# Loading operands already transposed by DMA in a two-problem attention kernel

## The chip, the cores and the metric

The kernel runs on one core of one Trainium2 chip. The metric is device time in microseconds for one launch of the whole program. A profile is one execution of the program recorded by the hardware profiler; its span runs from the first to the last instruction and its own measured time is a little longer.

## The reference, cut to what matters

Two independent problems share one launch. Each has 2048 tokens, 512 channels and 32 heads of 16 channels. Problem A is attention in four segments of 512 tokens with a causal mask inside the segment, mixed with a linear "memory" of all earlier segments. Problem B is plain attention over all 2048 tokens, without a mask.

```python
# A: q, k, v = x@wq, x@wk, x@wv, cut in N=4 segments of L=512; phi(t) = t+1 if t>0 else exp(t)
for s in range(N):
    qs, ks, vs = q[:, :, s], k[:, :, s], v[:, :, s]
    logits = einsum('bhqd,bhkd->bhqk', qs, ks) * Dh**-0.5 + mask
    a_dot = einsum('bhqk,bhkd->bhqd', softmax(logits), vs)
    a_mem = einsum('bhld,bhde->bhle', phi(qs), M) / (einsum('bhld,bhd->bhl', phi(qs), z)[..., None] + 1e-06)
    outs.append(g * a_mem + (1.0 - g) * a_dot)          # g = sigmoid(beta), one value per head
    M = M + einsum('bhld,bhle->bhde', phi(ks), vs)
    z = z + einsum('bhld->bhd', phi(ks))
a = concat(outs) @ wo_A
# B: q, k, v = split(x @ wqkv)
b = softmax(einsum('bhqd,bhkd->bhqk', q, k) * Dh**-0.5) @ v @ wo_B      # per head
return concatenate([a, b], axis=-1)
```

## The kernel before, in words

The work is cut into units: one unit is four heads by 512 query tokens. A has 32 units (4 segments by 8 head groups), B has 32 (4 query chunks by 8 head groups). The order is fixed in `useq`: the eight units of A's segment 0 first, then B's units with A's later segments spread between them.

In a unit, TensorE computes scores with keys on the partitions (a bank is 128 keys by 512 queries of one head), an exponential turns them into P, and TensorE multiplies P by V into one accumulator `acc`, where an extra column of ones in V gives the softmax denominator. `finalize` then transposes and divides.

The exponentials of B are shared between two engines. ScalarE takes tiles of two or three banks from the PSUM tiles `s_ps` (`act_tile_b`, line 752; A's masked tiles are in `act_tile_a`, lines 678 to 688). VectorE takes one bank at a time from the two PSUM banks `d_ps` (`dve_bank`, scores on line 793) and builds an approximation of the exponential in three terms: line 804 writes the first term into the tile `pD`, and line 770 adds constants to make the other two. So a bank on VectorE needs three P-times-V products (line 906) with V scaled three ways (`VD`), where a bank on ScalarE needs one.

The instruction order on every engine is written out at build time by a planner: a loop in `fast_path` keeps a model clock `c["t"]` for TensorE and others for ScalarE, VectorE and GpSimd, and emits whatever its model says can go next. Each engine then runs its own list strictly in order. `pick` moves a B bank from VectorE's list to ScalarE's when the model says VectorE is behind, so the split between the engines is a result of the planning. Projections and other side work are "chores" with due times, run through the two `d_ps` banks: `chore_q`, `chore_k`, `chore_v` (four matmuls each and one copy out by VectorE), `chore_out` (output projection), `chore_xT` (transposition of x), `chore_kphi`, `chore_macc` and `chore_am` (A's memory). When TensorE would idle, `flush` and `fill_idle` emit products with zeros.

The parts around the change:

- x is loaded in blocks of 128 tokens (`load_x`, tile `xin`, five buffers). `fill_xT` (line 298) transposes a block by four TensorE products with the identity into a `d_ps` bank, and line 320 copies two blocks at a time to `xT_b` or `xT_a`. This is done eight times for B and six times for A's segments 1 to 3; A's segment 0 is done at the start.
- For the memory, phi(K) is needed with tokens on the partitions. `chore_kphi` projects K a second time in that layout, four chores per segment for three segments (line 333 with `wk_a`), copies it to `kb16` (line 424), and runs ScalarE's exp (line 431) and three GpSimd operations to make `phik`.
- All of these loads and the stores of the output (line 514) are issued from SyncE's queue.
- At the start, TensorE's list has the projections of the first q and k, then the q projection for the next two head groups (line 330, which needs the rest of `wq_a`), and only then the first scores of A (line 678).
- `PDB` is the number of `pD` buffers (3), and `QT_a`, the masked q of A, has three buffers.

Of the kernel before, what the change touches and what calls it, by code (L numbers as in the profile page):

```python
# [10 lines left out]
ALU = mybir.AluOpType  # L11
# [8 lines left out]
P = 128  # L20
# [21 lines left out]
def fast_path(ctx, tc, nc, A_x, A_wq, A_wk, A_wv, A_wo, A_beta, B_x, B_wqkv, B_wo, out, flag):  # L42
# [11 lines left out]
    PDB, PTB, XB = 3, 4, 5  # L54
# [13 lines left out]
    wv_b = sb_.tile([P, 4, D], BF16, name="wv_b", tag="phik", bufs=1)  # L68
# [3 lines left out]
    xorder = [("a", i) for i in range(4)] + [("b", i) for i in range(NSB)] + [("a", i) for i in range(4, NSB)]  # L72
    xtiles = {}
    xstate = dict(n=0)

    def load_x(upto, engs=(nc.sync,)):
        while xstate["n"] < min(upto, len(xorder)):
            k, i = xorder[xstate["n"]]
            xin = sb_.tile([P, D], BF16, name="xin", tag="xin", bufs=XB)
            src = xa2 if k == "a" else xb2  # L80
            engs[xstate["n"] % len(engs)].dma_start(out=xin[:], in_=src[i * P:(i + 1) * P, :])
            xtiles[(k, i)] = xin
            xstate["n"] += 1

    load_x(4, (nc.sync, nc.scalar))
# [46 lines left out]
    seg_v(0)  # L132
    beta_t = const.tile([P, HG], BF16, name="beta_t")
# [44 lines left out]
    load_x(5)  # L178
    nc.sync.dma_start(out=wv_b[:], in_=wview(B_wqkv)[:, :, 2 * D:3 * D])
    nc.sync.dma_start(out=wk_b[:], in_=wview(B_wqkv)[:, :, D:2 * D])  # L180
    nc.sync.dma_start(out=wq_b[:], in_=wview(B_wqkv)[:, :, 0:D])
# [104 lines left out]
    kphi_n = {}  # L286
    phik_t, phik_n, phik_at, mbd_at = {}, {}, {}, {}
# [7 lines left out]
    def fill_xT(bank, k, sbs):  # L295
        for n, i in enumerate(sbs):
            for cc in range(4):
                nc.tensor.transpose(bank[:, (4 * n + cc) * P:(4 * n + cc + 1) * P],  # L298
                                    xtiles[(k, i)][:, cc * P:(cc + 1) * P], ident[:])
        pe(60.0 * 4 * len(sbs), "full")  # L300

    def xT_tile(k, s):
        if (k, s) not in xT_t:
            if k == "a":
                xT_t[(k, s)] = sb_.tile([P, 4, 4, P], BF16, name="xT_a", tag="xT_a", bufs=1)
            else:
                for q in range(4):
                    xT_t[(k, q)] = None
                big = const.tile([P, NSB, 4, P], BF16, name="xT_b")
                for q in range(4):  # L310
                    xT_t[(k, q)] = big[:, 4 * q:4 * q + 4]
        return xT_t[(k, s)]

    def chore_xT(k, i0):
        load_x(xorder.index((k, i0)) + 2)
        bank = d_bank(BF16)
        c["t"] = max(c["t"], d_when())
        fill_xT(bank, k, (i0, i0 + 1))
        xt = xT_tile(k, i0 // 4)
        nc.vector.tensor_copy(xt[:, i0 % 4:i0 % 4 + 2], bank.rearrange("p (n c s) -> p n c s", n=2, c=4))  # L320
        d_done(dve_do(dve_cost(1024, 0.6), c["t"] + LAT))
        xT_made[(k, i0 // 4)] = xT_made.get((k, i0 // 4), 0) + 1
        del xtiles[(k, i0)], xtiles[(k, i0 + 1)]
        load_x(xorder.index((k, i0)) + 2 + XB)

    def proj(bank, w, wsl, xt, i=None):

        for cc in range(4):
            if i is None:
                nc.tensor.matmul(bank.rearrange("p (n s) -> p n s", n=4), w[:, cc, wsl], xt[:, :, cc, :],  # L330
                                 start=(cc == 0), stop=(cc == 3))
            else:
                nc.tensor.matmul(bank, xt[:, i, cc, :], w[:, cc, wsl], start=(cc == 0), stop=(cc == 3))  # L333
        pe(4 * MM, "full")
# [4 lines left out]
    def q_masks(k, s, rt, qc):  # L339

        t = sb_.tile([P, 2, 512], BF16, name=f"QT_{k}", tag=f"QT_{k}", bufs=3)
# [15 lines left out]
    def weights(k, what):  # L357
        if k == "a":
            return {"q": wq_a, "k": wk_a, "v": wv_a}[what][:]
        return {"q": wq_b[:], "k": wk_b[:], "v": wv_b[:]}[what]  # L360
# [11 lines left out]

    def chore_k(k, s, rt):
        def evac(bank):
            nc.vector.tensor_copy(k_dst(k, s, rt), bank)
            d_done(dve_do(dve_cost(512), c["t"] + LAT))
            k_ready[(k, s, rt)] = c["dve"] + LAT
        uses(k, s)
# [42 lines left out]
    def chore_kphi(s, i):  # L421
        def evac(bank):
            kb16 = sb_.tile([P, D], BF16, name="kb16", tag="kb16", bufs=2)
            nc.vector.tensor_copy(kb16[:], bank)
            d_done(dve_do(dve_cost(512), c["t"] + LAT))
            if i == 0:
                phik_t[s] = sb_.tile([P, 4, D], BF16, name="phik", tag="phik", bufs=1)

            def more():
                e = sb_.tile([P, D], BF16, name="ek", tag="e", bufs=2)  # L430
                nc.scalar.activation(e[:], kb16[:], ACT.Exp)
                act_do(act_cost(512) + 100, c["t"])
                nc.gpsimd.tensor_scalar(e[:], e[:], 1.0, 0.0, ALU.min, ALU.max)
                nc.gpsimd.tensor_scalar(kb16[:], kb16[:], 3e38, 0.0, ALU.min, ALU.max)
                nc.gpsimd.tensor_tensor(phik_t[s][:, i, :], kb16[:], e[:], op=ALU.add)
                gp_do(1024, c["act"] + LAT)
                gp_do(512, 0, 2.1)
                phik_at[(s, i)] = c["gp"] + LAT
                phik_n[s] = phik_n.get(s, 0) + 1
            at(c["dve"] + 400, more)  # L440
        uses("a", s)
        d_job(lambda b: proj(b, weights("a", "k"), slice(0, D), xT_tile("a", s), i), evac)
        kphi_n[s] = kphi_n.get(s, 0) + 1

    def chore_macc(s, half):
        def fill(bank):
            for r in range(2):
                rt = 2 * half + r
                for i in range(4):
                    nc.tensor.matmul(bank[:, r * 136:(r + 1) * 136], phik_t[s][:, i, rsl(rt)],  # L450
# [4 lines left out]
        def evac(bank):  # L455
# [13 lines left out]
            mbd_at[s] = c["gp"] + LAT  # L469
# [53 lines left out]
    def chore(need, fn, ok=None, due=None):  # L523
        chores.append(dict(due=due, need=need, fn=fn, ok=ok, n=len(chores)))

    def q_free(k, cc, rt):

        g = 4 * cc + rt - 3
# [12 lines left out]
    for rt in range(1, 4):  # L541
        n = begin("a", 0, 2 * rt)
        chore(n - 3000, lambda rt=rt: chore_k("a", 0, rt))
        chore(n - 4500, lambda rt=rt: chore_q("a", 0, rt))
    for g in range(4):
        n = b0 + 7400 * g
        for i in (0, 2):
            chore(n - 5500, lambda i=4 * g + i: chore_xT("b", i))
# [14 lines left out]
    for s in range(1, NSEG):  # L563
        n = begin("a", s, 0)
        for i in range(4):
            chore(n - 20000, lambda s=s, i=i: chore_kphi(s - 1, i),
                  ok=lambda s=s, i=i: (kphi_n.get(s - 1, 0) == i and phik_at.get((s - 1, i - 2), 0 if i < 2 else 1e18) <= now()
                                       and len(v_ready) >= NSB + 4))
        for half in range(2):
            chore(n - 10000, lambda s=s, half=half: chore_macc(s - 1, half),  # L570
                  ok=lambda s=s: phik_n.get(s - 1) == 4 and phik_at[(s - 1, 3)] <= now())
        for i in (0, 2):
            chore(n - 9000, lambda s=s, i=i: chore_xT("a", 4 * s + i),
                  ok=lambda s=s: xT_uses.get(("a", s - 1), 0) == (14 if s == 1 else 16))
# [1014 lines left out]
```

## Time and profile before

| what | value |
|---|---|
| median of 9 runs | 933.37 us (931.73 to 938.23) |
| time of the profiled execution | 931.37 us |
| its span | 929.6 us |
| TensorE matmul busy | 825.8 us (89%) |
| VectorE busy | 765.5 us (82%) |
| ScalarE busy | 862.3 us (93%) |
| GpSimd busy | 383.5 us (41%) |
| mean granted TensorE clock | 0.984 |
| data moved by DMA | 13.98 MB, mean 15 GB/s |

Busy times of the engines overlap, so they do not add up to the span. TensorE's 89% are modelled from pipelined matmuls, many of them four side by side in different columns or rows of the array, so it is not TensorE at its peak. The profiled execution lies 2.0 us below the median of the runs.

### The profile page before, as it was taken

To read this page: it belongs to the slowest core of one execution; us is meant where nothing else is said; L and a number is where in the kernel's file an instruction comes from. 1 tells how busy PE (TensorE), PEld (TensorE's weight loads), DVE (VectorE), ACT (ScalarE), POOL (GpSimd) and SP (SyncE) were. 2 spreads that over 40 slices of the span, in tenths; PEclk is the share of its full clock that TensorE was granted. 3 is DMA by queue.
4 is the path that set the end of the run, shared out by engine and by line. 5 is a ranking of instruction groups with operands and counts; after the bars stand their busy time and mean duration, and the time that the engine had idled before them with its cause. 6 is when DMAs were issued, how large, how long until landed. Compare 5 with 4: busy or idle time off the path is not lost.

```text
span 929.6 us, 20299 instructions
## 1 busy us (share of the span) xinstructions
PE 825.8 (89%) x8083; PEld 269.5 (29%) x8083; DVE 765.5 (82%) x1540; ACT 862.3 (93%) x804; POOL 383.5 (41%) x772
## 2 busy tenths in 40 slices
PE   5999999898989889999988988899889888988976
PEld 2333322232322223222322222232222223322222
DVE  3564589989998888589889799978898899989895
ACT  2999999999999988899999999999999999999995
POOL 3860734352433356236343333575333153533130
PEclk7999999999999998999999999999999999999999
DMA  7011000000000000000000000000000000000000
GB/s 228 29 46 47 23 2 1 1 2 1 1 2 18 7 1 14 18 13 1 2 1 2 23 1 2 1 2 24 2 1 1 24 1 1 2 1 2 24 1 28
DMA packets 14729, 13.98 MB, mean 15 GB/s; under 512 B 2336, under 2 KB 14624, under 8 KB 14624
## 3 DMA queue, kind: packets, MB, share of 16 engines
q1 hardware_dynamic: 13392, 11.93, 4.1%
q8 instruction: 65, 1.06, 0.5%
q10 hardware_dynamic: 1104, 0.66, 0.2%
q14 instruction: 40, 0.33, 0.1%
q0 software_dynamic: 128, 0.00, 0.0%
HBM read 8.39 MB, written 4.19 MB: 14 GB/s over the span
## 4 chain that ended last, share of the span: by engine, by line
PE 35%; ACT 26%; DVE 20%; issue 13%; POOL 5%; DMA 1%; ACTq 0%; DVEq 0%
ACT pT L752 24%; PE acc L906 11%; DVE pD L804 7%; PE s_ps L747 7%; DVE pD L770 6%; PE d_ps L330 4%; PE d_ps L333 3%; DVE tT L840 2%; PE s_ps L678 2%; POOL pT L699 2%; PE d_ps L500 2%; PE d_ps L793 2%; ACT pT L688 2%; DMA wq_a<-in_A_wq_dram 1%; PE d_ps L298 1%
## 5 line engine op out<-in xcount | busy, mean ns | idle before, releaser
L752 ACT ACTIVATE pT<-s_ps 128x1536 bf16<-128x1536 f32 (+2 forms) x614 | 695.2, 1237 | 30.6 <-PE s_ps L747 18.6
L804 DVE TENSOR_SCALAR pD<-d_ps 128x512 int16<-128x512 f32 x546 | 355.3, 676 | 24.4 <-PE d_ps L793 22.6
L747 PE MATMUL s_ps<-QT_b,KT_b 32*128 32x512 bf16 x1502 | 239.9, 385 | 46.6 <-ACT pT L752 40.7
L906 PE MATMUL acc<-pT,VP_b 128*32 128x512 bf16 x1502 | 249.3, 385 | 0.5 <-ACT pT L752 0.5
L770 DVE TENSOR_SCALAR pD<-pD 128x1024 int16<-128x1024 int16 (+1 forms) x562 | 244.4, 478 | 0.8
L906 PE MATMUL acc<-pD,VD 128*32 128x512 f16 x1638 | 232.5, 387 | 3.1 <-DVE tT L840 2.0
L793 PE MATMUL d_ps<-QT_b,KT_b 32*128 32x512 bf16 x546 | 194.0, 382 | 17.2 <-DVE pD L804 14.2
L699 POOL TENSOR_SCALAR_AFFINE_SELECT pT<-pT 128x512 bf16<-128x512 bf16 (+3 forms) x192 | 96.1, 518 | 235.9 <-ACT pT L688 234.2
L688 ACT ACTIVATE pT<-s_ps 128x1280 bf16<-128x1280 f32 (+1 forms) x128 | 138.8, 1137 | 19.6 <-PE s_ps L678 16.8
L747 PEld LDWEIGHTS <-KT_b 32*128 32x128 bf16 x1502 | 74.1, 91 | 247.6 <-issue 234.0
L906 PEld LDWEIGHTS <-VD 128*32 128x32 bf16 x1638 | 56.4, 95 | 85.1 <-issue 72.6
L621 POOL TENSOR_SCALAR VD<-VP_b 128x288 bf16<-128x288 bf16 (+1 forms) x186 | 71.0, 382 | 13.1
L840 DVE STREAM_TRANSPOSE tT<-acc 128x512 f32<-128x512 f32 x64 | 45.5, 711 | 37.1 <-PE acc L906 35.5
L906 PEld LDWEIGHTS <-VP_b 128*32 128x32 bf16 x1502 | 58.8, 95 | 53.6 <-issue 38.8
L343 POOL TENSOR_SCALAR QT_a<-qc,mq 128x512 bf16<-128x512 bf16 x30 | 21.4, 724 | 110.8 <-DVE qc L399 110.8
L678 PE MATMUL s_ps<-QT_a,KT_a 32*128 32x384 bf16 (+3 forms) x512 | 57.4, 303 | 7.3 <-ACT pT L688 3.7
L992 PE MATMUL acc<-wq_a,zero 128*32 128x256 bf16 (+1 forms) x908 | 60.7, 292 | 2.9 <-DVE tT L840 2.5
L793 PEld LDWEIGHTS <-KT_b 32*128 32x128 bf16 x546 | 44.3, 91 | 19.7 <-issue 18.8
L343 POOL TENSOR_SCALAR QT_b<-qc,mq 128x512 bf16<-128x512 bf16 x32 | 22.8, 724 | 53.6 <-DVE qc L401 53.2
L906 PE MATMUL acc<-pT,VP_a 128*32 128x384 bf16 (+3 forms) x512 | 39.6, 311 | 4.0 <-POOL pT L699 3.4
L992 PEld LDWEIGHTS <-zero 128*32 128x32 bf16 x924 | 23.5, 94 | 54.2 <-issue 50.3
L861 POOL TENSOR_TENSOR tN<-tT,RA 128x256 bf16<-128x256 f32 x31 | 21.4, 689 | 38.2 <-DVE RA L843 38.2
(120 smaller groups left out, 679.1 us busy)
## 6 DMA issues: line engine op xcount, KB each, us to landing
out_dram<-osb SPq DMA_DIRECT2D x30, 128.0 KB, 1.7
xin<-in_B_x_dram SPq DMA_DIRECT2D x16, 128.0 KB, 2.2
xin<-in_A_x_dram SPq DMA_DIRECT2D x14, 128.0 KB, 2.3
wv_a<-in_A_wv_dram SPq DMA_DIRECT2D x1, 512.0 KB, 9.0
wv_b<-in_B_wqkv_dram SPq DMA_DIRECT2D x1, 512.0 KB, 9.0
wk_b<-in_B_wqkv_dram SPq DMA_DIRECT2D x1, 512.0 KB, 9.6
wq_b<-in_B_wqkv_dram SPq DMA_DIRECT2D x1, 512.0 KB, 8.5
wo_a<-in_A_wo_dram SPq DMA_DIRECT2D x1, 512.0 KB, 8.2
```

The costliest lines, as they stand in the source:

```text
L621: mul = lambda dst, src: nc.gpsimd.tensor_scalar(dst, src, EXP_C[k], 1.0, ALU.mult, ALU.mult)
L678: nc.tensor.matmul(pt[:, b, col:col + w], kt[32 * j:32 * j + 32, kbl * P:(kbl + 1) * P], q[32 * j:32 * j + 32, P * kbl:512], start=(r == 0 ...
L688: nc.scalar.activation(pT[:].rearrange("p b n -> p (b n)")[:, 0:n], pt[:].rearrange("p b n -> p (b n)")[:, 0:n], ACT.Exp, scale=0.25)
L699: nc.gpsimd.affine_select(out=blk, in_=blk, compare_op=ALU.is_ge, fill=0.0, base=0, pattern=[[0, e - b], [0, w // P], [1, P]], channel_mul ...
L747: nc.tensor.matmul(pt[:, b, :], KT_b[32 * j:32 * j + 32, u["rt"], kb * P:(kb + 1) * P], q[32 * j:32 * j + 32, :], start=True, stop=True, t ...
L752: nc.scalar.activation(pT[:, 0:n, :], pt[:, 0:n, :], ACT.Exp, scale=1.0 / (LOG2E * 1024.0))
L770: nc.vector.tensor_scalar(tile[:, k, 0:n, :], tile[:, 0, 0:n, :], EXP_D[k], None, ALU.add)
L793: nc.tensor.matmul(bank, KT_b[32 * j:32 * j + 32, u["rt"], kb * P:(kb + 1) * P], qslice(u)[32 * j:32 * j + 32, :], start=True, stop=True, ...
L804: nc.vector.tensor_scalar(pd[:, 0, n, :], bank, EXP_B, 0.0, ALU.add, ALU.max)
L840: nc.vector.transpose(tT[:].rearrange("p c d -> p (c d)"), u["acc"][:])
L906: nc.tensor.matmul(u["acc"][32 * j:32 * j + 32, e["c0"]:512], e["lhsT"], e["rhs"], start=(j not in u["started"]), stop=False, tile_positio ...
L992: nc.tensor.matmul(bank[32 * j:32 * j + 32, 0:w], zero[:, 0:32], wq_a[:, 0, 0:w], start=fresh, stop=False, tile_position=(0, 32 * j), skip ...
```

## The change

It has five parts.

1. x of B is loaded by four DMA transposes of 512 by 512 elements straight from DRAM into `xT_b`, issued from SyncE's queue between the loads of B's weights. x of A's segments 1 to 3 comes by one such transpose each. The loads, the TensorE transposes and the copies for them go; A's segment 0 is done as before.
2. phi(K) starts from a DMA transpose of `KT_a` (K as the scores use it, 128 by 512, in SBUF) into `phik`, 12 in all; the second K projection and its copies go. ScalarE's exp and GpSimd's operations on `phik` stay. `phik` uses four buffers.
3. `PDB` goes from 3 to 5, `QT_a` from 3 buffers to 2; `wv_b` and two late scratch tiles move to other buffers.
4. The first scores of A come ahead of all projections but the first q and k: chores of segment 0 wait for `scount[0] >= 5`, that is for three score tiles.
5. The planner's rules change in places: a VectorE bank goes ahead of a chore when VectorE is about to run dry, `ENDW` goes from 700 to 400, the memory chores `chore_am` come due 1 us earlier of the planner's clock, and a unit of A waits for its memory part before it is finalized.

```diff
-    PDB, PTB, XB = 3, 4, 5
+    PDB, PTB = 5, 4
+    QTB = dict(a=2, b=3)
...
-    load_x(5)
-    nc.sync.dma_start(out=wv_b[:], in_=wview(B_wqkv)[:, :, 2 * D:3 * D])
-    nc.sync.dma_start(out=wk_b[:], in_=wview(B_wqkv)[:, :, D:2 * D])
-    nc.sync.dma_start(out=wq_b[:], in_=wview(B_wqkv)[:, :, 0:D])
+    xT_b = const.tile([P, 4, S], BF16, name="xT_b")
+    for q in range(4):
+        nc.sync.dma_start_transpose(out=xT_b[:, :, q * 512:(q + 1) * 512], in_=xb2[q * 512:(q + 1) * 512, :])
+        w, part = ((wq_b, 0), (wk_b, 1), (wv_b, 2), (None, 0))[q]
+        if w is not None:
+            nc.sync.dma_start(out=w if w is wv_b else w[:], in_=wview(B_wqkv)[:, :, part * D:(part + 1) * D])
     nc.sync.dma_start(out=wo_a[:], in_=wview(A_wo))
     nc.sync.dma_start(out=wo_b[:], in_=wview(B_wo))
...
-    def chore_xT(k, i0):
...
+    def chore_xT(s):
+        nc.sync.dma_start_transpose(out=xT_tile("a", s), in_=xa2[s * 512:(s + 1) * 512, :])
+        xT_made[s] = c["t"] + 9000
...
+    def phi_k(s, rt):
+        kn = phik_t[(s, rt)] = sb_.tile([P, 4, P], BF16, name="phik", tag="xin", bufs=4)
+        nc.sync.dma_start_transpose(out=kn[:], in_=KT_at[(s, rt)][:])
+        def more():
+            e = sb_.tile([P, 4, P], BF16, name="ek", tag="e", bufs=2)
+            nc.scalar.activation(e[:], kn[:], ACT.Exp)
...
+        at(c["dve"] + 12000, more)
...
-    def chore_kphi(s, i):
...
-        chore(n - 3000, lambda rt=rt: chore_k("a", 0, rt))
-        chore(n - 4500, lambda rt=rt: chore_q("a", 0, rt))
+        chore(n - 3000, lambda rt=rt: chore_k("a", 0, rt), ok=lambda rt=rt: scount[0] >= 5 and q_free("a", 0, rt))
+        chore(n - 4500, lambda rt=rt: chore_q("a", 0, rt), ok=lambda rt=rt: scount[0] >= 5 and q_free("a", 0, rt))
...
-    LATE, SLK, EVEN, ENDW = 470.0, 400.0, 2, 700
+    LATE, SLK, EVEN, ENDW = 470.0, 400.0, 2, 400
...
+    at(t0 + 6000, lambda: phi_k(0, 0))
...
+            if u["k"] == "a" and u["c"] > 0 and u["am"] is None:
+                for x in chores:
+                    if x.get("am") is u:
+                        x["due"] = -1.0
+                order_chores()
+                break
...
+                first = (du is not None and c["dve"] < t + 700 and not stalled and not blocked
+                         and ch is not None and prog[0] < ch["due"] + 4000)
+                if first and room >= MM + DR:
+                    dve_bank(du)
+                    continue
```

Read from the two built programs, the change of instruction counts is as follows. "Columns" are the 512 queries of a bank.

| engine | instructions | before | after |
|---|---|---|---|
| ScalarE | exponential over three banks / two / one (line 752 before) | 294 / 300 / 20 | 287 / 295 / 17 |
| VectorE | first term `pD` from `d_ps` (line 804 before) | 546 | 580 |
| VectorE | other terms, two banks / one (line 770 before) | 530 / 32 | 560 / 40 |
| VectorE | copies `xT_a`, `xT_b`, `kb` | 7, 8, 12 | 1, 0, 0 |
| TensorE | 128x128 transposes of x | 128 | 16 |
| TensorE | K projection for the memory, matmuls | 48 | 0 |
| TensorE | P times V, ScalarE's P of B / VectorE's | 1502 / 1638 | 1468 / 1740 |
| SyncE | DMA transposes | 0 | 19 |
| SyncE | loads of x | 30 | 2 |

## The prediction

> **What bounds the kernel now.** I read the page's busy shares first, then busy time by stretch, then the waits of ScalarE, then the rows of the groups with shapes kept apart, and last the start of the timeline.
>
> ```profile
> PE 825.8 (89%) x8083; PEld 269.5 (29%) x8083; DVE 765.5 (82%) x1540; ACT 862.3 (93%) x804; POOL 383.5 (41%) x772
> ```
>
> ScalarE is idle for 929.6 - 862.3 = 67.3 us. Where that idle time lies is in the stretches (columns: stretch, its length, then busy us of PE, PEld, DVE, ACT, POOL, then clock):
>
> ```profile
> 0.00:23.20 23.20, 13.66 (x56) 5.25 (x57) 7.16 (x35) 5.52 (x6) 9.05 (x37) 0.78 0.73 228
> 200.00:300.00 100.00, 90.21 (x936) 29.22 (x932) 91.64 (x186) 96.72 (x90) 39.57 (x80) 1.00 0.02 5
> 300.00:400.00 100.00, 91.99 (x800) 28.73 (x792) 79.61 (x150) 90.15 (x86) 46.96 (x90) 0.91 0.04 10
> 400.00:500.00 100.00, 89.95 (x958) 28.89 (x961) 88.98 (x186) 97.10 (x90) 36.99 (x75) 1.00 0.01 3
> ```
>
> In the long middle ScalarE is 96 to 97% busy with VectorE at about 89%: ScalarE sets the pace, so its work counts nearly one to one. The two big holes are the first 23.2 us (17.7 us idle) and the last 29.6 us (12.6 us idle). A smaller one is 300:400 (9.9 us idle, clock 0.91). The waits of ScalarE say who ends its idle time:
>
> ```profile
> ACT pT L752 <- PE s_ps L747: 18.6, 33, 1.9
> ACT pT L688 <- PE s_ps L678: 16.8, 17, 9.7
> ACT pT L752 <- PE d_ps L793: 7.8, 19, 1.0
> ```
>
> The longest single wait, 9.7 us, is before the first tile of A. The timeline shows why:
>
> ```profile
> 5.62 0.88 SPq L177 DMA_DIRECT2D wq_a<-in_A_wq_dram  x1
> 8.27 0.58 ACT L948 CAST KT_a<-s_ps 128x512 bf16<-128x512 f32 x1 [2.60 <-PE s_ps L330]
> 16.05 1.89 PE L330 MATMUL d_ps<-xT_a,wq_a 128*128 128x512 bf16 x4 [7.82 <-DMA wq_a<-in_A_wq_dram]
> 18.53 2.15 ACT L688 ACTIVATE pT<-s_ps 128x1280 bf16<-128x1280 f32 x2 [9.68 <-PE s_ps L678]
> ```
>
> The first keys are ready at 8.85 us, but TensorE's next instruction is a projection whose weights land at 16.05, and the first scores stand behind it.
>
> **The change part by part.** The durations:
>
> ```profile
> L752 ACT ACTIVATE pT<-s_ps 128x1536 bf16<-128x1536 f32 x294 | 432.4, 1471 | 25.6 <-PE s_ps L747 15.8 <-PE d_ps L793 6.4 <-POOL tN L861 0.2
> L752 ACT ACTIVATE pT<-s_ps 128x1024 bf16<-128x1024 f32 x300 | 313.1, 1047 | 5.0 <-PE s_ps L747 2.7 <-PE d_ps L793 1.4
> L804 DVE TENSOR_SCALAR pD<-d_ps 128x512 int16<-128x512 f32 x546 | 355.3, 676 | 24.4 <-PE d_ps L793 22.6
> L770 DVE TENSOR_SCALAR pD<-pD 128x1024 int16<-128x1024 int16 x530 | 236.0, 487 | 0.8
> L424 DVE CAST kb<-d_ps 128x512 bf16<-128x512 f32 x12 | 8.2, 687 | 6.0 <-PE d_ps L333 6.0
> L320 DVE COPY xT_b<-d_ps 128x1024 bf16<-128x1024 bf16 x8 | 5.3, 669 | 1.6 <-PE d_ps L298 1.6
> ```
>
> *ScalarE's share.* 34 banks move to VectorE: 7 x 1.471 + 5 x 1.047 + 3 x 0.646 (the one-bank row) = 17.5 us less. On the pacing engine: **-17.5 us**.
>
> *VectorE.* It gains 34 x 0.676 + 30 x 0.487 + 8 x 0.339 (the one-bank row of line 770) = 40.3 us, and loses 12 x 0.687 and 14 copies of x (8 x 0.669, 6 x 0.681) = 17.7 us. 765.5 + 22.6 = 788 us, about 86% of a span near 915; in the middle it goes from 89 to about 92% of the time. This lies beside ScalarE. What it costs is waits: with two `d_ps` banks, TensorE stands before line 793 until VectorE has emptied one, and ScalarE's next scores queue behind. That wait is 7.8 us today. Bounds: 0 (five `pD` buffers and VectorE-first scores help) to about 12 us, if it and VectorE's part of the s_ps wait grow by half. I take **+2**, because VectorE still keeps 8% of slack.
>
> *TensorE.* Gone are 112 transposes (16 of them take 1.86 us: 13 us) and 48 projection matmuls (four take 1.04 us: 12.5 us); 68 more P-times-V products come, four side by side at 387 ns, so 6.6 us. Net about -19 us, off the path: cover is ScalarE. I count nothing, though less full-array work in 300:400 could return a few of its 9.9 us.
>
> *ScalarE's exp and GpSimd's three operations for phi(K)* stay, 12 each. Part 5's rules, and `QT_a` with two buffers, show only in the order; a late mask of q costs at most 0.72 us (line 343) at 12 later pairs of A units, 0 to 8 us. I put it in the range, not in the sum, since q's chores are issued 3 to 5 us of the planner's clock ahead.
>
> *First scores.* TensorE's new list has three score tiles, then the V projection, which waits for `wv_a` (issued 4.58, landing 9.0 us later: 13.6). So ScalarE does tiles 1 to 3 (3.5 us of work) from about 9.0 to 12.5, waits, and has tile 4 at about 15.5: the 1.0 to 1.9 us of that projection and a tile of scores come between. Before, the first tile began at 18.53. Work done and moment together: 18.5 - (15.5 - 3.5) = **-6.5 us**.
>
> *DMA transposes, the new wait.* SyncE's queue now holds, after `wq_a` (16.05): four transposes of 512 KB, wq_b, wk_b, wv_b, wo_a, wo_b, and behind all of these the first transposes of `KT_a`. In ScalarE's list the first exp of `phik` stands behind 15 tiles, three A units. If it has not landed, every later tile queues behind that exp, P-times-V behind the tiles, and VectorE's fourth `KT_a` copy waits for the same DMA to release its buffer. By ScalarE's time the exp is due at 15.5 + (15.5 - 3.5) x 1.09 = 28.6 (a unit is 5.2 us: rows 1.244, 1.244, 1.031, 1.031, 0.606; 1.09 is the idle it has in 23:46). The DMA: the five weight loads behind it landed about 1.45 us apart (issue plus time to landing: 8.9 + 9.0 = 17.9 for wv_b to 15.3 + 8.5 = 23.8 for wo_b), so 16.05 + 5 x 1.45 + 4T + 2.3 (a 128 KB load from issue to landing) = 25.6 + 4T, where T is the time of one 512 KB transpose. The stall is **4T - 3**.
>
> T isn't in the trace. The nearest row is the plain load of the same bytes, 1.45 us. Two rules of the Trainium skill bear on it and disagree. "DMA: Bandwidth & Descriptors", section "Latency and other measured facts", has 261 GB/s for a DMA transpose on one kernel, so 2.0 us (estimate): a stall of 5. "VectorE: DVE Perf Modes", section "The three transpose paths", speaks against the change: 1309 ns by DMA against 390 ns on TensorE for a 128x128 block (TensorE's row here is 219 ns). If 16 blocks ran one after another, that is 21 us for 512 KB (estimate): a stall of 81 us. The one rule gives a gain of 17 us, the other a loss of 59. I take T = 2.5, near the plain load's row: **+7**. Ends: 1.45 (+2.8) and 21 (+81); below nothing it can't be, since the same bytes move. B's consumers are safer: `wq_b` and the first quarter of x are due after 17.8 us of ScalarE's work, at about 31, and land at about 16 + T + 1.5. The later xT_a are issued long ahead; SyncE otherwise waits 711.6 us for output copies, so its queue is free.
>
> Sum: -17.5 + 2 - 6.5 + 7 = -15 us. From the span 929.6 that gives 914.6, or 916.4 with the 1.8 us around it, against 931.37 for the same execution. The median is 2.0 above that execution, so **918.4, rounded to 918**.
>
> **The rivals.** *VectorE becomes the pace.* For: 92% in the middle, and it runs its list in order with two banks. Against: 8% left, five `pD` buffers. If the d_ps waits eat 9 to 12 of the 17.5 us, with the late masks: about 926 (923 to 930). Chance 0.20.
>
> *The transposes are slow, and the start stands still.* This is the other side: the exp of `phik` at the head of ScalarE's list. The stall exceeds the gain of 22 us when 4T - 3 > 22, T above about 6.2 us (85 GB/s); a transpose of `KT_a` that takes much longer than a load adds itself, four times in a row at the start. For: the code leaves 9 us of its clock for a 512 KB transpose and 12 for one of `KT_a`, and nothing in the trace proves it fast. Against: the plain load's row. With T = 9: 33 us of stall, about 944; with 21, about 992. Chance 0.26.
>
> *It evens out*, T of 5.5 to 6.5: 931 to 936. Chance 0.07. That the transposes were not issued, or the banks not moved, is excluded by the built lists.
>
> **How the numbers follow.** The sum's own case has 0.47, range 907 to 924. A measurement here can tell about 0.3% (2.8 us) from no change. Faster by more than that: 0.47 + 0.20 = 0.67; within: 0.07; slower: 0.26. The range goes from 907 (T = 1.45, no waits, some of 300:400 back) to 948, which leaves out the slower half of the slow case (0.13) and little below.
>
> **What would show it.** Right: first ScalarE tile near 9 us; ScalarE busy near 845 us; one wait of ScalarE on the phik DMA of 3 to 11 us before 45 us; 512 KB transposes about 2 to 3 us apart; VectorE near 788. Wrong: DMA waits of tens of us in the first 100 us; exps of `phik` waiting in later segments too; ScalarE below 94% in 400:900 with TensorE waiting for line 804's successor.

## The result, and the profile after

The changed kernel has a median of 922.57 us (10 runs, 917.68 to 930.6), the kernel before 933.51 us in the runs beside it. The slowest run, 930.6 us at a granted clock of 0.953, counts as a slow one and is left out of the ratio. The ratio is 0.9882, with an interval of 0.986 to 0.9904: 1.2% faster, at a median 4.6 us above the forecast of 918 us. The profiled execution of the changed kernel took 915.76 us, with a span of 913.9, where the prediction's sum had 914.6.

The first row of the page:

```profile
PE 799.9 (88%) x8107; PEld 254.3 (28%) x8107; DVE 782.1 (86%) x1586; ACT 844.0 (92%) x789; POOL 384.2 (42%) x772
```

ScalarE has 862.3 - 844.0 = 18.3 us less work. Its idle time went from 67.3 to 913.9 - 844.0 = 69.9 us. So 18.3 - 2.6 = 15.7 us came off the span: the work taken off ScalarE, nearly whole, and nothing from its waits. The stretches (columns as before: stretch, length, busy us of PE, PEld, DVE, ACT, POOL, clock) show that the holes did not close:

```profile
0.00:23.20 23.20, 16.26 (x100) 6.12 (x100) 7.16 (x35) 9.60 (x10) 9.90 (x39) 0.85 0.81 180
...
200.00:300.00 100.00, 88.75 (x944) 28.78 (x942) 95.38 (x194) 96.17 (x91) 42.29 (x80) 1.00 0.03 7
300.00:400.00 100.00, 89.93 (x875) 27.26 (x875) 83.90 (x164) 91.23 (x85) 47.03 (x95) 0.93 0.06 16
400.00:500.00 100.00, 86.04 (x941) 26.43 (x937) 93.84 (x192) 94.71 (x88) 39.98 (x75) 0.98 0.01 3
```

VectorE is now as full as ScalarE in 200:300 and nearly so in 400:500. ScalarE does about 4 us more in the first 23.2 us than before, but not for long: by 93 us it has been busy for 69.64 us, against 71.31 before. The waits of ScalarE over the whole span (total us, times, longest):

```profile
ACT pT L726 <- PE d_ps L767: 16.0, 32, 2.5
ACT pT L662 <- PE s_ps L652: 14.8, 20, 4.0
ACT pT L726 <- PE s_ps L721: 11.3, 20, 2.2
```

Line 726 is line 752 of before, 662 is 688, 767 is 793. The wait behind VectorE's banks doubled, from 7.8 to 16.0 us, and the wait for its own scores fell from 18.6 to 11.3: together within 1 us of before. No row for the DMA of `phik` is among them.

### The profile page after: what moved, and what is told of

Same layout as the page of the kernel before. It is cut to its first block, busy times and chain, and to the rows that moved or that the text cites. A ratio compares the mean times of both kernels' runs of the same rounds, so it can differ in the third digit from the quotient of the medians.

```text
span 913.9 us, 20345 instructions
## 1 busy us (share of the span) xinstructions
PE 799.9 (88%) x8107; PEld 254.3 (28%) x8107; DVE 782.1 (86%) x1586; ACT 844.0 (92%) x789; POOL 384.2 (42%) x772
## 4 chain that ended last, share of the span: by engine, by line
DVE 26%; ACT 25%; PE 25%; issue 12%; POOL 10%; DMA 1%; ACTq 0%; DVEq 0%
ACT pT L726 24%; DVE pD L778 11%; PE acc L881 9%; DVE pD L744 8%; PE s_ps L721 5%; POOL pT L673 4%; PE d_ps L315 3%; DVE tT L815 2%; PE d_ps L482 2%; PE d_ps L767 2%; PE s_ps L652 2%; ACT pT L662 1%; PE d_ps L317 1%; POOL VD L595 1%; DMA wq_a<-in_A_wq_dram 1%
## 5 line engine op out<-in xcount | busy, mean ns | idle before, releaser
L726 ACT ACTIVATE pT<-s_ps 128x1536 bf16<-128x1536 f32 (+2 forms) x599 | 678.4, 1246 | 30.9 <-PE d_ps L767 16.0
L778 DVE TENSOR_SCALAR pD<-d_ps 128x512 int16<-128x512 f32 x580 | 374.9, 675 | 17.1 <-PE d_ps L767 15.6
L721 PE MATMUL s_ps<-QT_b,KT_b 32*128 32x512 bf16 x1468 | 235.3, 388 | 53.4 <-ACT pT L726 45.1
L744 DVE TENSOR_SCALAR pD<-pD 128x1024 int16<-128x1024 int16 (+1 forms) x600 | 262.9, 480 | 0.9
L881 PE MATMUL acc<-pD,VD 128*32 128x512 f16 x1740 | 236.8, 393 | 5.2 <-DVE tT L815 4.3
L881 PE MATMUL acc<-pT,VP_b 128*32 128x512 bf16 x1468 | 235.2, 391 | 0.0
L767 PE MATMUL d_ps<-QT_b,KT_b 32*128 32x512 bf16 x580 | 209.3, 386 | 19.3 <-DVE pD L778 16.5
L662 ACT ACTIVATE pT<-s_ps 128x1024 bf16<-128x1024 f32 (+1 forms) x128 | 137.8, 1154 | 16.6 <-PE s_ps L652 14.8
L652 PE MATMUL s_ps<-QT_a,KT_a 32*128 32x512 bf16 (+3 forms) x512 | 56.6, 302 | 11.3 <-ACT pT L662 4.2
L767 PEld LDWEIGHTS <-KT_b 32*128 32x128 bf16 x580 | 46.1, 91 | 16.7 <-issue 15.3
L881 PE MATMUL acc<-pT,VP_a 128*32 128x512 bf16 (+3 forms) x512 | 40.6, 305 | 4.4 <-POOL pT L673 3.8
```

Source lines behind the costliest of these rows:

```text
L652: nc.tensor.matmul(pt[:, b, col:col + w], kt[32 * j:32 * j + 32, kbl * P:(kbl + 1) * P], q[32 * j:32 * j + 32, P * kbl:512], start=(r == 0 ...
L662: nc.scalar.activation(pT[:].rearrange("p b n -> p (b n)")[:, 0:n], pt[:].rearrange("p b n -> p (b n)")[:, 0:n], ACT.Exp, scale=0.25)
L721: nc.tensor.matmul(pt[:, b, :], KT_b[32 * j:32 * j + 32, u["rt"], kb * P:(kb + 1) * P], q[32 * j:32 * j + 32, :], start=True, stop=True, t ...
L726: nc.scalar.activation(pT[:, 0:n, :], pt[:, 0:n, :], ACT.Exp, scale=1.0 / (LOG2E * 1024.0))
L744: nc.vector.tensor_scalar(tile[:, k, 0:n, :], tile[:, 0, 0:n, :], EXP_D[k], None, ALU.add)
L767: nc.tensor.matmul(bank, KT_b[32 * j:32 * j + 32, u["rt"], kb * P:(kb + 1) * P], qslice(u)[32 * j:32 * j + 32, :], start=True, stop=True, ...
```

## The experiments

Each kernel was timed beside the kernel before. The number "at equal clock" in the table needs a word. Within each kernel the runs differ by how long TensorE was granted half its speed: 2 x (1 - granted clock) x span. A straight line through each kernel's own runs has slopes of 0.17 to 0.35 us per us of it, mostly 0.22 to 0.31. The column gives each line's value at 30 us of half-clock time. Only before, e1, e3, e7 and e12 have runs on both sides of 30 us; for all others the line reaches beyond every run of theirs, furthest for e5 (75 us and more) and e2 (59 and more). The column also does not show that the clock is the cause: a run that waits more gives TensorE more gaps.

The medians have a second limit. The kernel before had 933.5 us beside the changed kernel and 930.8 to 931.6 us beside the others, so medians from different sets compare to 2 or 3 us only. The ratios do not have this fault, and where it matters both are given.

| kernel | ratio to before, interval | median us | median clock | at equal clock |
|---|---|---|---|---|
| before | 1 | 930.8 to 933.5 | 0.979 to 0.983 | about 930 |
| after | 0.9882, 0.986 to 0.9904 | 922.57 | 0.970 | 915.7 |
| e1 guard of the first scores, on before | 1.0017, 0.9996 to 1.0038 | 932.32 | 0.9795 | 930.1 |
| e2 after without that guard | 1.0027, 1.0004 to 1.0051 | 933.81 | 0.961 | 921.0 |
| e3 after with three `pD` buffers | 0.9966, 0.9947 to 0.9985 | 927.84 | 0.981 | 926.7 |
| e4 the transposes alone | 1.0067, 1.0046 to 1.0088 | 937.28 | 0.975 | 932.0 |
| e5 after, 16 more transposes at the start | 1.0325, 1.0282 to 1.0368 | 960.63 | 0.951 | 945.8 |
| e6 after, gate masks later | 0.9911, 0.9874 to 0.9947 | 924.65 | 0.967 | 914.7 |
| e7 after, more zero products | 0.9853, 0.9814 to 0.9891 | 915.49 | 0.9805 | 913.5 |
| e8 after, planner's `LATE` 475 | 0.9908, 0.9873 to 0.9943 | 920.63 | 0.969 | 913.5 |
| e9 transposes and five `pD` buffers | 0.9901, 0.9863 to 0.9939 | 920.11 | 0.9715 | 914.8 |
| e10 before with four `pD` buffers, no transposes | 0.9959, 0.994 to 0.9978 | 926.73 | 0.9765 | 924.3 |
| e11 before with e7's zero products | 0.9977, 0.9954 to 1.0 | 929.83 | 0.9915 | 933.9 |
| e12 after, still more zero products | 0.9932, 0.9906 to 0.9959 | 923.98 | 0.986 | 924.9 |

### The guard of the first scores, alone and taken away (e1, e2)

```diff
# e1, on the kernel before (the same for chore_q)
-        chore(n - 3000, lambda rt=rt: chore_k("a", 0, rt))
+        chore(n - 3000, lambda rt=rt: chore_k("a", 0, rt), ok=lambda: scount[0] >= 5)
# e2, on the kernel after (the same for chore_q)
-        chore(n - 3000, lambda rt=rt: chore_k("a", 0, rt), ok=lambda rt=rt: scount[0] >= 5 and q_free("a", 0, rt))
+        chore(n - 3000, lambda rt=rt: chore_k("a", 0, rt), ok=lambda rt=rt: q_free("a", 0, rt))
```

> The kernel before with one part of the change: chores of A's segment 0 wait until three score tiles are out. The split stays at 1502 banks on ScalarE and 546 on VectorE. If the first scores are worth what the prediction says, the first tile of A begins near 9 to 13.5 us instead of 18.5 and the run is 4 to 6.5 us shorter (ratio 0.993 to 0.996). The rival: the wait only moves, since the q of the next heads is now projected and masked later, so ScalarE stands again before the third unit and the run is within 2 us of before (ratio 0.998 to 1.002).

e1 is no faster than before. ScalarE's timeline in e1 shows where the early start goes:

```profile
9.70 2.15 ACT L688 ACTIVATE pT<-s_ps 128x1280 bf16<-128x1280 f32 x2 [0.55 <-PE s_ps L678]
17.75 1.24 ACT L688 ACTIVATE pT<-s_ps 128x1280 bf16<-128x1280 f32 x1 [5.89 <-PE s_ps L678]
...
31.25 4.20 ACT L688 ACTIVATE pT<-s_ps 128x1280 bf16<-128x1280 f32 x4 [4.03 <-PE s_ps L678]
```

The first tile starts at 9.70 instead of 18.53, but two tiles later ScalarE waits 5.89 us, and before the third unit another 4.03. The first tile of B starts at 61.98 us against 63.00 before: 1 us of the 8.8 is left. In the changed kernel the first tile of B starts at 65.64 us, with four exps of `phik` (2.5 us) ahead of it that come after 97 us in the kernel before: nothing of the early start is left there either.

> The changed kernel without the guard on segment 0's chores (1474 banks on ScalarE, 574 on VectorE). If the first scores are worth 4 to 6.5 us: about 927 to 929. The rival, that the wait only moves: within 2 us of the changed kernel, 921 to 925, with the first tile of A late again and no 4 us wait of ScalarE at 26 to 31 us.

Without the guard the median is 11 us higher (1.5% by the ratios), where e1 had made the guard worth nothing. About half of that goes with the clock (0.961 against 0.970): at equal clock it is 921.0 against 915.7, both beyond their runs. e9 below has no guard either and is as fast as the changed kernel, so it is not the early scores that carry those 5 us, but presumably something in the order that the planner makes without them, under part 5's rules. What it is stays open.

### The transposes alone, and the buffers (e4, e3, e9, e10)

```diff
# e4, on the kernel after: the guard of e2 goes too, and three of part 5's four rules
-    PDB, PTB = 5, 4
-    QTB = dict(a=2, b=3)
+    PDB, PTB = 3, 4
+    QTB = dict(a=3, b=3)
...
-                chore(u["at"] + 2000, lambda u=u: chore_am(u), am=u,
+                chore(u["at"] + 3000, lambda u=u: chore_am(u), am=u,
...
-    LATE, SLK, EVEN, ENDW = 470.0, 400.0, 2, 400
+    LATE, SLK, EVEN, ENDW = 470.0, 400.0, 2, 700
...
-                if first and room >= MM + DR:
-                    dve_bank(du)
-                    continue
# e3, on the kernel after
-    PDB, PTB = 5, 4
+    PDB, PTB = 3, 4
# e9, on e4
-    PDB, PTB = 3, 4
-    QTB = dict(a=3, b=3)
+    PDB, PTB = 5, 4
+    QTB = dict(a=2, b=3)
```

> The kernel with the DMA transposes alone: no guard on the first scores, three pD buffers, three QT_a buffers, and the planner's old rules (no VectorE bank ahead of a chore, ENDW 700, memory chores at the old due time). The split is 1490 and 558: 12 banks moved of 34. If ScalarE's load alone sets the gain, 12 banks of 0.46 us give 5.5 us: about 928. If what the transposes take off TensorE and VectorE is worth more than the banks it lets move, 924 or less. If the TensorE clock is what the removed full-array work kept up, the mean granted clock falls below 0.975 and the gain is smaller: 930 or more.

The fourth rule of part 5, by which a unit of A waits for its memory part, stays in e4 and e9. The transposes alone make the kernel 0.7% slower. In e4's profile ScalarE is busy for 854.1 us, 8.2 less than before. The planner gave VectorE 12 more banks of B (558 for 546), which by the rows of before is 6.3 us of it (two tiles each of three, two and one bank). But it idles for 929.7 - 854.1 = 75.6 us, 8.3 more, and the span stays at before's 929.6 (the median is above before's, for the most part with a lower clock: at equal clock 2 us). So what was taken off TensorE and ScalarE came back as waits of ScalarE.

> The changed kernel with three pD buffers instead of five; the planner's split is 1471 on ScalarE and 577 on VectorE, almost the same. If the buffers themselves keep VectorE from waiting, VectorE's idle time and TensorE's waits before its scores grow and the run is 3 us or more longer (926 or more). The rival: five buffers do next to nothing, 921 to 925.

Five buffers against three inside the whole change are worth 927.84 - 922.57 = 5 us of median, 8 us by the ratios, and 11 us at equal clock.

> The DMA transposes and five pD buffers (with two of QT_a), without the guard on the first scores and with the planner's old rules; split 1477 and 571. The transposes alone with three buffers gave 937. If the buffers carry the gain, this comes to 922 to 927. The rival: the buffers only help together with the new rules, and it stays at 930 or more.

e9 is e4 with five `pD` buffers and one `QT_a` buffer less, and it has all of the gain within the intervals: 920.11 us, a ratio of 0.9901 against 0.9882, without the guard and without three of part 5's rules. Against e4 its profiled span is 14.7 us shorter: 5.9 us less work on ScalarE (848.2) and 8.8 us less idle (66.8). The middle, 93 to 890 us, of before, e4, e3, e9 and the changed kernel in this order (columns as above; VectorE is the third busy time, ScalarE the fourth):

```profile
93.00:890.00 797.00, 716.77 (x7188) 231.49 (x7189) 692.84 (x1382) 764.35 (x710) 329.19 (x651) 0.99 0.02 7
```
```profile
93.00:890.00 797.00, 707.24 (x7168) 223.86 (x7166) 695.79 (x1391) 758.78 (x705) 315.54 (x630) 0.99 0.03 8
```
```profile
93.00:890.00 797.00, 714.01 (x7337) 226.64 (x7336) 714.23 (x1437) 757.62 (x699) 318.56 (x627) 0.99 0.03 8
```
```profile
93.00:890.00 797.00, 702.12 (x7342) 223.12 (x7388) 714.81 (x1435) 765.38 (x713) 330.78 (x645) 0.99 0.03 8
```
```profile
93.00:890.00 797.00, 703.64 (x7381) 222.06 (x7380) 726.15 (x1459) 762.48 (x708) 324.92 (x632) 0.98 0.03 8
```

With three buffers, e3 puts as much work on VectorE as e9 does, but ScalarE is held to 757.6 us of it; with five, both engines are full at once (714.8 and 765.4). What differs is TensorE. It has as many instructions in e9 as in e3 and is busy for 12 us less. Its P-times-V products alone (line 881), in the same stretch, in e3 and in e9:

```profile
93.00:890.00 797.00, 307.92 (x3436) 82.29 (x3436) 0.99 0.03 8
```
```profile
93.00:890.00 797.00, 274.82 (x3448) 72.68 (x3447) 0.99 0.03 8
```

The same products take 33 us less, 80 ns each instead of 90. All the kernels sort by their buffers in this: 87 to 90 ns with three (before, e1, e4, e3), 81 with four (e10), 79 to 83 with five (e9, after, e7, e8, e12, and e2 with 83 at the lowest clock). A busy time counts products that run side by side once, and one product of B lasts as long in both (388 to 392 ns), so in e9 more of them run side by side. In the code a round of products (`flush`) takes one for each of the four heads that has one ready. That more buffers have more of them ready, and so fill the rounds, is argued. VectorE's wait for its scores, which falls from 33.5 us in e3 to 8.2 in e9, is no such sign: it is 22.6 in the kernel before with three buffers and 21.4 in e7 with five.

```diff
# e10, on the kernel before, with the guard, two QT_a buffers and two of part 5's rules
-    PDB, PTB, XB = 3, 4, 5
+    PDB, PTB, XB = 4, 4, 4
...
-    LATE, SLK, EVEN, ENDW = 470.0, 400.0, 2, 700
+    LATE, SLK, EVEN, ENDW = 470.0, 400.0, 2, 400
...
+                if first and room >= MM + DR:
+                    dve_bank(du)
+                    continue
```

> The kernel before (x and phi(K) by loads, TensorE and VectorE) with the rest of the change: four pD buffers, two of QT_a and four of xin (all that fits beside the old tiles), the guard on the first scores, VectorE's bank ahead of a chore, ENDW 400. The planner gives 1478 and 570 banks. If the transposes count only for the SBUF they free, this has most of the gain: 922 to 927. If the work that they take off TensorE and VectorE is needed to make the moved banks pay, VectorE (24 banks more, nothing removed) runs dry less but stands longer in TensorE's way: 929 or more.

e10 has no transpose at all and is 0.4% faster than before: about a third of the gain. It also has the guard, which e1 measured at nothing, and two of the rules, which were not run alone. One buffer of `pD` is 6 KB of each partition. The changed kernel has 12 KB more of them, and gives up 9 KB of other tiles: 4 of `phik`, 2 of `kb16`, one `xin` and 2 of `QT_a`. The first three, 7 KB, go with the old loads and the second projection. e10 keeps those tiles and comes to the same total with four buffers, with `XB` at 4 and two buffers of `QT_a`; whether other tiles could have made room for a fifth was not tried. So in these runs the transposes paid only together with the memory that they free. How much of the distance from e10 to the changed kernel is the fifth buffer, and how much TensorE's smaller load, is not told apart: the transposes with four buffers were not run, and e10 has the shorter products (81 ns) while its ScalarE does only 754.6 us in the middle (in a profiled run that was the slowest of its twelve).

### The other side's mechanism, made real (e5)

```diff
+    hold = sb_.tile([P, 4, P], BF16, name="hold", tag="osb", bufs=2)
+    for q in range(16):
+        nc.sync.dma_start_transpose(out=hold[:], in_=xb2[q * P:(q + 1) * P, :])
```

These sixteen transposes of 128 KB stand behind the load of `wo_b` and ahead of the first transposes of `KT_a`; nothing reads `hold`.

> The changed kernel with the same plan on every engine, but 16 more DMA transposes of 128x512 in SyncE's queue right before the first transposes of KT_a, so that phik lands later at the start and nowhere else. If the prediction's stall term is right (ScalarE stands at the first exp of phik until it has landed, and the time is never made up), phik lands some 16 to 40 us later, ScalarE shows one wait on that DMA of about the same length less a few us, and the run grows by that wait: 935 to 955. The rival: ScalarE's later idle time absorbs part of it, and less than half of the wait shows in the end.

ScalarE's timeline of e5:

```profile
75.13 0.63 ACT L367 ACTIVATE ek<-phik 128x512 bf16<-128x512 bf16 x1 [39.41 <-DMA phik<-KT_a]
```

The wait of 39.41 us is paid whole: the median is 38 us above the changed kernel's, 41 us by the ratios, and the profiled span 41.3. The number at equal clock, 30 us above, says little here, since the wait itself lowers the clock: in 46 to 93 us, while TensorE is busy for only 15.77 of 47 us, the granted clock is 0.63. So the mechanism that the prediction feared is as it said; in the changed kernel it only lacked the size.

### The gate masks out of the way of q's (e6)

```diff
-        for par in range(2):
+    def setup_masks():
+        for par in range(2):
             to = maskg[:].rearrange("p (r t) j d -> p t r j d", t=2)[:, par]
...
+    at(t0 + 30000, setup_masks)
```

> The changed kernel with the same plan, but GpSimd's ten products for the memory's mask (maskg) are put some 20 us later in its list. In the changed kernel they stand, with three mask operations, ahead of the two that make the q of the second pair of units, and ScalarE waits 4.0 us there. If that list order is what holds ScalarE, the wait falls to about 1.5 us and the run is 2 to 3 us shorter (ratio 0.985 or a little below). The rival: the wait moves to the next q or to P times V, and the run is within 1 us of the changed kernel's.

In the changed kernel GpSimd makes eight gate masks between 25.87 and about 28 us, then three selects, and only then the q mask that TensorE's next scores need:

```profile
25.87 1.04 POOL L154 TENSOR_TENSOR maskg<-jm,mqg 128x64 f32<-128x64 f32 x4 [0.43 <-DVE mqg L148]
27.04 1.04 POOL L154 TENSOR_TENSOR maskg<-jm,mqg 128x64 f32<-128x64 f32 x4
28.04 1.26 POOL L673 TENSOR_SCALAR_AFFINE_SELECT pT<-pT 128x512 bf16<-128x512 bf16 x3
29.30 1.37 POOL L327 TENSOR_SCALAR QT_a<-qc,mq 128x512 bf16<-128x512 bf16 x2
```

e6 takes the masks away from there. ScalarE's timeline of e6:

```profile
28.36 4.20 ACT L664 ACTIVATE pT<-s_ps 128x1280 bf16<-128x1280 f32 x4 [2.33 <-PE s_ps L654]
...
34.69 0.63 ACT L366 ACTIVATE ek<-phik 128x512 bf16<-128x512 bf16 x1 [1.65 <-DMA phik<-KT_a]
```

The wait fell from 4.03 to 2.33 us, and 1.65 us of it came back at once at the phik DMA, which had been hidden behind the first wait. At equal clock e6 is within 1 us of the changed kernel.

### Another plan, and more zero products (e8, e7, e11, e12)

```diff
# e8, on the kernel after
-    LATE, SLK, EVEN, ENDW = 470.0, 400.0, 2, 400
+    LATE, SLK, EVEN, ENDW = 475.0, 400.0, 2, 400
# e7 on the kernel after, e11 on the kernel before; e12 on after with 2600
-    GAP, SPAN, WARM = 120, 1700, 2000
+    GAP, SPAN, WARM = 120, 1700, 2300
```

> The changed kernel with one constant of the planner moved by 1% (LATE 475 instead of 470), which means nothing by itself but makes another plan from early on (split 1467 and 581). It measures how much of any difference here is only the luck of a plan. If the parts' effects of 5 to 11 us are effects of the parts, this stays within 2 us of the changed kernel at the same half-clock time. The rival: plans differ by 5 us and more for no reason, and single parts can't be told from luck.

This one nudge to a constant of the planner moves the time by about 2 us: at least that much is luck of the plan, and differences of this size between the other kernels are not read.

> The changed kernel with more products with zeros on TensorE where the planner sees it idle (threshold 2300 instead of 2000: 1727 such products instead of 1227; split 1469 and 579). In the runs so far time and granted clock move together: 0.22 to 0.29 us for each us at half clock, where the half-clock time is 2 x (1 - clock) x span. If half-clock time costs ScalarE its scores, the granted clock rises from 0.970 to above 0.98 and the median falls by 4 to 7 us, to 916 to 919. The rival: the products stand in front of scores and take back what the clock gives: 921 or more.

The kernel fills TensorE's gaps with products by zero; `WARM` sets how many. In the changed kernel the clock falls to half for windows of about 3.4 us, one of them 10.2, after stretches in which TensorE had gaps. One of them, us by us (the first busy time is TensorE's, the third column from the end the clock):

```profile
428.00:429.00 1.00, 0.24 (x4) 0.00 (x0) 1.00 (x3) 1.00 (x2) 0.00 (x0) 1.00 0.00 0
429.00:430.00 1.00, 1.00 (x9) 0.22 (x8) 1.00 (x4) 0.60 (x1) 0.00 (x0) 0.54 0.00 0
430.00:431.00 1.00, 1.00 (x12) 0.14 (x8) 1.00 (x3) 0.79 (x1) 0.00 (x0) 0.50 0.00 0
431.00:432.00 1.00, 1.00 (x14) 0.24 (x10) 0.92 (x3) 0.94 (x2) 0.00 (x0) 0.50 0.00 0
432.00:433.00 1.00, 1.00 (x13) 0.12 (x5) 0.00 (x0) 0.74 (x1) 0.00 (x0) 0.76 0.00 0
433.00:434.00 1.00, 0.93 (x8) 0.20 (x7) 1.00 (x2) 0.97 (x1) 0.00 (x0) 1.00 0.03 8
```

With 2300, e7's median clock rises from 0.970 to 0.9805 and its median is 915.49 us, the lowest of all and 1.5% under before. By its median it is 7 us under the changed kernel, by the ratios 0.3%, and the two intervals overlap.

> The kernel before with the raised threshold for products with zeros (2300; 1695 of them instead of 1088 to 1111; split 1503 and 545). Its clock is 0.979 to 0.983 already, some 32 to 39 us at half clock. If half-clock time costs 0.27 us per us, at most 8 us can be won; with the fall that the changed kernel had (20 us of half clock) 5 us: 925 to 928. If the changed kernel gained from it only because the change itself had lowered its clock, before stays at 929 to 933.

> The changed kernel with a threshold of 2600 (2419 products with zeros; split 1478 and 570). More of the same: if half-clock time is what is left to win, clock near 0.985 and 912 to 916. If the added products begin to stand in front of scores, 917 or more, above the threshold of 2300.

More zero products are no general cure. On the kernel before the clock rises to 0.9915, but the median gains only 1.4 us: at equal clock the kernel is 4 us worse, presumably by the products themselves. With 2600 on the changed kernel the clock is 0.986 and the median 923.98, 8 us above e7's (0.8% by the ratios). There the planner also gave ten banks of B back to ScalarE (1478 where the changed kernel has 1468), presumably because the products left less room in TensorE's list. Between 2000 and 2600 only 2300 was tried.

## Why the prediction was right

*ScalarE's share: right in size, and the whole of the gain.* Predicted 17.5 us less, measured 18.3. So close a hit is part luck: the same sum over tiles gives 6.3 for e4, where 8.2 were measured, and 16.7 for e3, where it was 15.3. And the prediction gave it to the 34 banks as if they were free to move. e4 shows that they are not: with three buffers, work moved to VectorE came back as waits. e9 shows that the five buffers carry it. The prediction named them only as a reason for small waits, and counted 6.6 us more of TensorE's time for the 68 added products. With the five buffers all P-times-V products took 279.4 us in the middle instead of 291.8, and TensorE's busy time fell by 25.9 us, not 19.

*VectorE and its waits: right in sum, wrong in the term.* Its busy time is 782.1 us (predicted 788). Taken as +2, the waits at `d_ps` alone are +8; the waits for ScalarE's own scores gave 7 of them back. The prediction's rival, VectorE as the pace, is half there: in 200:300 VectorE is 95% busy beside ScalarE's 96%.

*First scores: the step that failed by its size, -6.5 predicted.* e1 measures 1 us of it left at the first tile of B, and nothing in the median. The prediction had three score tiles in a row ahead of the V projection. TensorE's timeline of the changed kernel has something between the second and the third:

```profile
13.10 0.50 PE L652 MATMUL s_ps<-QT_a,KT_a 32*128 32x512 bf16 x5 [0.68 <-ACT KT_a L920]
15.70 0.96 PE L965 MATMUL acc<-wq_a,zero 128*32 128x256 bf16 x20 [2.10 <-DMA wq_a<-in_A_wq_dram]
16.59 0.60 PE L652 MATMUL s_ps<-QT_a,KT_a 32*128 32x128 bf16 x5
```

and e8, whose first tile was early:

```profile
8.91 0.50 PE L652 MATMUL s_ps<-QT_a,KT_a 32*128 32x512 bf16 x5 [0.68 <-ACT KT_a L920]
15.39 1.26 PE L965 MATMUL acc<-wq_a,zero 128*32 128x256 bf16 x20 [5.98 <-DMA wq_a<-in_A_wq_dram]
16.58 0.61 PE L652 MATMUL s_ps<-QT_a,KT_a 32*128 32x128 bf16 x5
```

Twenty zero products, there to keep TensorE busy, read 256 columns of `wq_a`, of which only the first 128 are loaded early. They wait for the rest of it, until about 15.5 us, and the third tile's scores stand behind them. So the fourth tile of ScalarE starts at 19.59 (predicted 15.5), whether the first starts at 9.35 (e8) or at 13.54 (the changed kernel, where the first block of `wq_a` took 7.3 us to land). A zero product that reads something loaded early should mend this; it was not tried. The second piece is the wait of 4.03 us for the q mask, which the prediction did not have (its late masks, in the range at 0.72 us each, were those of later pairs); it is in e1 too, so it comes with the early start and not with the transposes.

*The phik stall: wrong by its size the other way, +7 predicted, 0 measured.* The landing was right, the due time was not. SyncE's queue in the changed kernel, with the time that each entry held it (the last row is four entries of 1.19 us each, with the waits between them):

```profile
8.37 7.05 SPq L173 DMA_TRANSPOSE xT_b<-in_B_x_dram  x1
15.47 0.57 SPq L176 DMA_DIRECT2D wq_b<-in_B_wqkv_dram  x1
16.09 3.54 SPq L173 DMA_TRANSPOSE xT_b<-in_B_x_dram  x1
...
29.04 0.51 SPq L178 DMA_DIRECT2D wo_b<-in_B_wo_dram  x1
29.65 15.34 SPq L360 DMA_TRANSPOSE phik<-KT_a  x4
```

`wo_b` landed 5.1 us after its issue, at 34.1, and the rest of `wq_a` at 15.64. With five weight loads at 1.45 us between them, the four transposes took (34.1 - 15.64 - 5 x 1.45) / 4 = 2.8 us each, where T = 2.5 was taken. Landing by landing they took 1.8 to 3.4 us each, 2.4 on average, and the weight loads 1.8. The first data of `phik` were there at 29.65 + 5.2 (from issue to landing, the longest of the twelve) = 34.85, where 35.6 was predicted; in e6, whose exp waits for them, it starts at 34.69. ScalarE came to the exp at 35.08 instead of 28.6, because of the two waits above, and found it ready:

```profile
30.54 4.20 ACT L662 ACTIVATE pT<-s_ps 128x1280 bf16<-128x1280 f32 x4 [4.03 <-PE s_ps L652]
34.60 0.63 ACT L659 ACTIVATE pT<-s_ps 128x512 bf16<-128x512 f32 x1
35.08 0.66 ACT L364 ACTIVATE ek<-phik 128x512 bf16<-128x512 bf16 x1
```

The two terms were coupled: had ScalarE come to the exp at 28.6, it would have waited there for about 6 us. e6 shows it, where less of the one wait brought the other. That is why -6.5 and +7 both being wrong left the sum right. The prediction had not seen the coupling, so that its sum of 914.6 met the span of 913.9 so closely is luck.

*The two rules weighed for T.* The estimate from the Trainium skill's "DMA: Bandwidth & Descriptors", section "Latency and other measured facts" (2.0 us for 512 KB at 261 GB/s), was 0.4 to 0.8 us too low. The one from "VectorE: DVE Perf Modes", section "The three transpose paths" (21 us, if 16 blocks of 1309 ns ran one after another), was far off. Even 2.8 us is under the 6.2 from which the slow case decides, and e5 shows what that case would have been.

*From span to median: not in the prediction.* It put the median 2.0 us above the profiled execution, as before. It is 922.57 - 915.76 = 6.8. The changed kernel's runs have a median clock of 0.970, and the profiled one had 0.979. That is 55 against 38 us of half-clock time, and by this kernel's slope of 0.27 it makes 4.5 of the 6.8 us. Before's runs beside the experiments have 32 to 39 us. So the change goes with a lower clock: if the slope is taken for the price, the median would be some 5 us lower at before's clock. That this comes from TensorE's gaps, now that 112 transposes and 48 projection products are gone, is argued; that the clock can be had back is shown by e7.

## What to carry to other kernels

Work taken off an engine that does not set the pace was worth nothing by itself here, and work moved to a second engine paid only with enough buffers between that engine and the TensorE that both share: cost the memory that a change frees, and what it buys. When a start is made earlier, follow each engine's list to the next wait, fillers and masks included, since a filler has inputs too; two waits in a row for one engine are not added but the later one taken. Look at the granted clock, and at the kernel before in the same set of runs, before a difference of a per cent is given a reason.

## What the runs showed of the hardware that was not expected

- A DMA transpose of 512 KB from DRAM held SyncE's queue for 3.42 to 7.05 us at the crowded start and for 1.70 to 2.22 us later (the three of `xT_a`); the plain loads of 512 KB between the first ones held it for 0.51 to 0.58. At the start a transpose landed 1.8 to 3.4 us after the entry ahead of it, a plain load 1.3 to 2.4. The transposes of `KT_a` from SBUF (128 KB) held the queue for 1.19 us and landed 2.4 us after their issue, the first one 5.2.
- Among the runs of one kernel, 1 us more of half-clock time went with 0.17 to 0.35 us more of time, in a kernel that ScalarE paces. Filling the gaps with zero products raised the clock each time, but not the speed: by the ratios e7 (clock 0.9805) is 0.3% faster than the changed kernel (0.970), e12 with still more of them (0.986) 0.5% slower.
- The same P-times-V products took 87 to 90 ns of TensorE's time each with three `pD` buffers and 79 to 83 with five, though one product lasted as long (385 to 395 ns, and about 400 in e2, whose clock was lowest).
- The first load of 128 KB of `wq_a` took 7.3 us to land in the one execution profiled after and 3.9 in the one before. e8, with the same loads, had its first keys at 8.27 us as before: this varies between executions, and here cost nothing.
